# Attention weights turned by VectorE and transfers instead of TensorE, in a top-k attention and feed-forward kernel

## The chip, the cores and the metric

The kernel runs on one core of a Trainium2 chip. The metric is the device time of one execution in microseconds (us). PE is TensorE, DVE is VectorE, ACT is ScalarE, POOL is GpSimd, and SP is SyncE, which here only issues transfers. PEld is the weight load of PE.

## The reference

Attention with the 32 largest scores of each row, then a feed-forward block on its result:

```
B, H, S, D = 8, 8, 576, 64
scores = q @ k.T / 8                      # per batch and head, 576 x 576
kth    = 32nd largest score of the row
attn   = softmax(where(scores >= kth, scores, -1e9))
x      = (attn @ v), heads side by side   # 4608 x 512
h      = x @ w_in                         # 512 x 2048
out    = (h - tanh(h)) @ w_out            # 2048 x 512
```

q, k and v are float32. The two weight matrices lie in memory as float64, and the kernel turns them into float32 itself. All matmuls are float32.

## The kernel before

**Steps.** The attention is cut into 144 steps. A step (class Step: batch b, head pair hp, query tile qt) takes two heads and 128 query rows of each. A batch has 16 such steps (four head pairs, four query tiles) and two remainder steps (qt = 4, `rem`), in which the last 64 query rows of four heads share one tile. So a batch is 18 steps. The order is written out by hand in `plan`: the half a = 0 (query tiles 0 and 1 of all head pairs, eight steps), then the two remainder steps, then a = 1. Two steps with the same hp and neighbouring qt make a pair, and `values` works once per pair.

**What a step does.** `scores` makes scps with PE (L202) and copies it to sc with ACT (L210). `search` finds the 32nd largest on DVE: it folds the two halves of a row into a maximum and a minimum (L232, L233), and makes four rounds of MAX8 (L240) and MATCH_REPLACE8 (L243), three of the latter. `mask` computes the threshold on POOL (tbs L259, nb L268), subtracts a huge multiple of what lies below it (ACT L272, POOL L275), and keeps b8s (L277) for a test at the end of whether the fold lost anything. `expo` takes the exponential in place in z on ACT (L288) with its row sum den, and POOL adds a small number (rd L302). `invert` is the reciprocal on DVE (L309) once per pair, and `spread` widens it on POOL (rx L319).

**Turning the weights.** z has queries on the partitions; the product with v needs keys there. `weigh` does that on PE: eight 128 x 128 transposes into PSUM (zt L341), copied by ACT to et (L344), and one more for the last 64 keys of both heads (L347, copied to e4 by L348). `values` multiplies with v (av L368), transposes rx beside it (L376), copies both (xs L380) and multiplies them on POOL into the unit's xT (L390, or L385 for a remainder).

**Feed-forward.** A unit is 256 finished rows of x: two per batch, and one of remainder rows for every four batches, 18 in all. `values` of a unit's last step (dictionary `done`) puts the unit's work items on a list: 16 of `ffn_h` (hps L410; every second one followed by tanh L422, copy L423 and subtraction L424) and 16 of `ffn_o` (ops L430, copy ot L440, store L442). `deal` takes items from the list inside the loop over steps, in four places of a step, so many that the list is empty when the next unit is due (`share`).

**The loop.** Every engine works through its instructions in the order in which the loop writes them. Iteration n holds `weigh` for step n-2, `mask` for n-1, `search` for n, items, `scores` for n+1, the end of `weigh`, `expo` for n-1, items, `values` for n-2, items, and then loads (`todo`): k and q of the next head pair, turned by DVE in 32 x 32 blocks (`turn_kq` L186), and v (L176, L180).

**Converting the weight matrices.** In the first 17 steps (EARLY) `search` is interleaved with 32 pieces of `convert`. A piece is loaded twice by ACT's queue, as raw (L119) and with an offset as shifted (L121), three places each. Its first part is two operations on DVE (L131, L135) and three on ACT (L132, L133, L138); its second part is one on DVE (L141) and one on POOL (L144). After a piece's second part the piece three further on is loaded. `between(i)` is called after round i of a search and runs what is planned there: one piece per step in steps 0 to 8, four in step 9, three in the steps after it.

```
seq = [(1, i) for i in mine[:1]]
for i in mine[1:]:
    seq += [(1, i), (2, i - 1)]
seq += [(2, i) for i in mine[-1:]]
for x, (part, i) in enumerate(seq):
    parts.setdefault((m, 3 * x // max(len(seq) - 1, 1)), []).append((part, i))
```

Of the kernel before, what the change touches and what calls it, by code (L numbers as in the profile page):

```python
# [42 lines left out]
def kernel(  # L43
# [21 lines left out]
    NG = P // G  # L65
    WJ = 4
# [22 lines left out]
    rawpool = pool("raw", 3)  # L89
    shpool = pool("shifted", 3)  # L90
# [13 lines left out]
    NW = 512  # L104
    e1151 = consts.tile([P, 1], FP32, name="e1151")
# [4 lines left out]
    def convert(j, i):  # L110


        if j < WJ:
            src, dst = moe_w_in[i * P : (i + 1) * P, j * NW : (j + 1) * NW], w_in[j][:, i, :]
        else:
            r0 = ((j - WJ) * FJ + i) * P
            src, dst = moe_w_out[r0 : r0 + P, :], w_out[j - WJ][:, i, :]
        raw = rawpool.tile([P, NW, 2], U32, tag="raw", name="raw")
        nc.scalar.dma_start(raw[:].rearrange("p n w -> p (n w)"), src.bitcast(U32))  # L119
        shifted = shpool.tile([P, NW, 2], U32, tag="shifted", name="shifted")  # L120
        nc.scalar.dma_start(  # L121
            shifted[:].rearrange("p n w -> p (n w)").bitcast(U8)[:, 0 : 8 * NW - 4],
            src.bitcast(U8)[:, 3 : 8 * NW - 1],
        )
        yield
        hi = raw[:, :, 1]
        f = thpool.tile([P, NW], FP32, tag="th", name="f")
        fu = f[:].bitcast(U32)


        nc.vector.tensor_scalar(fu, hi, 20, 0x7FF, ALU.logical_shift_right, ALU.bitwise_and)  # L131
        nc.scalar.activation(f[:], fu, AF.Relu, bias=e1151[:], scale=-(2.0**23))  # L132
        nc.scalar.activation(f[:].bitcast(I32), f[:], AF.Relu, bias=e255[:], scale=-1.0)  # L133

        nc.vector.tensor_scalar(  # L135
            dst.bitcast(U32), shifted[:, :, 0], 0x0FFFFFFF, None, ALU.bitwise_and
        )
        nc.scalar.activation(dst, dst.bitcast(U32), AF.Copy, bias=1.0, scale=2.0**-28)  # L138
        yield

        nc.vector.scalar_tensor_tensor(  # L141
            out=fu, in0=hi, scalar=0x80000000, in1=fu, op0=ALU.bitwise_and, op1=ALU.bitwise_or
        )
        nc.gpsimd.tensor_tensor(dst, dst, f[:], ALU.mult)  # L144
        yield
# [101 lines left out]
    tbs = consts.tile([P, 2, B * NHP * J + 2 * B], FP32, name="tbs")  # L247
    b8s = consts.tile([P, 2, B * NHP * J + 2 * B], FP32, name="b8s")

    def mask(n, exact):  # L250
# [3 lines left out]
        scf = sc[:].rearrange("p t s k -> p t (s k)")  # L254
        if exact:
            nc.gpsimd.tensor_scalar(tbs[:, :, n], m[:, :, TOP - 1], BIG, None, ALU.mult)
        else:
            for t in range(2):
                nc.gpsimd.tensor_scalar(  # L259
                    tbs[:, t, n : n + 1],  # L260
                    m[:, t, TOP - 1 : TOP],
                    m[:, t, TOP - 9 : TOP - 8],
                    BIG,
                    ALU.min,
                    ALU.mult,
                )
# [4 lines left out]
        for t in range(2):  # L271
            nc.scalar.activation(  # L272
                zv[:, t, :], scf[:, t, :], AF.Relu, bias=tbs[:, t, n : n + 1], scale=-BIG
            )
            nc.gpsimd.tensor_tensor(zv[:, t, :], scf[:, t, :], zv[:, t, :], ALU.subtract)  # L275
        if not exact:
            nc.gpsimd.tensor_scalar(  # L277
                b8s[:, :, n], x.pop("ab")[:, :, S2 + 7], BIG, None, ALU.mult
            )
# [41 lines left out]
    ets = {}  # L321

    def weigh(n):


        g, z = steps[n], st[n]["z"]
        if g.rem:
            o = 0
        else:
            o = (g.qt % 2) * P  # L330
        if o:
            et, e4 = ets[n - 1]
        else:
            et = etpool.tile([P, 2, J, N], FP32, tag="et", name="et")
            e4 = etpool.tile([P, N], FP32, tag="e4", name="e4")
        ets[n] = et, e4
        for t in range(2):
            zt = zt_ps.tile([P, 512], FP32, tag="zt", name="zt")
            m0 = t * (S + R)
            for c in range(J):  # L340
                nc.tensor.transpose(  # L341
                    zt[:, c * P : (c + 1) * P], z[:, m0 + c * P : m0 + (c + 1) * P], ident[:]
                )
            nc.scalar.copy(et[:, t, :, o : o + P], zt[:].rearrange("p (c j) -> p c j", c=J))  # L344
        yield
        zt = zt_ps.tile([P, 512], FP32, tag="zt", name="zt")
        nc.tensor.transpose(zt[:, 0:P], z[:, JP : JP + P], ident[:])  # L347
        nc.scalar.copy(e4[:, o : o + P], zt[:, 0:P])  # L348
        st.pop(n)
        yield  # L350

    def values(n):
# [4 lines left out]
        et, e4 = ets.pop(n)  # L357
        ets.pop(n - 1, None)
        rx = rxs.pop(n)
        nq = 1 if g.rem else 2  # L360
        w = nq * P
        av = zt_ps.tile([P, 2, N], FP32, tag="zt", name="av")
        for i in range(2 if g.rem else 1):
            cols = half(i) if g.rem else slice(0, N)
            hp = g.hp + i
            for c in range(J + 1):
                for t in range(2):
# [3 lines left out]
                        et[:, t, c, cols] if c < J else e4[:, cols],  # L371
# [3 lines left out]
        for i in range(nq):  # L375
            nc.tensor.transpose(  # L376
                av[:, 1, i * P : (i + 1) * P], rx[:, i].rearrange("p t d -> p (t d)"), ident[:]
# [10 lines left out]
        else:  # L388
            u = units[g.b, g.qt // 2]
            nc.gpsimd.tensor_tensor(xt(u)[:, g.hp, :], xs[:, 0], xs[:, 1], ALU.mult)  # L390
# [65 lines left out]
    def plan():  # L456
# [8 lines left out]
        for b in range(B):  # L465
# [3 lines left out]
            for a in range(2):  # L469
# [3 lines left out]
                done[len(steps) - 1] = units[b, a]  # L473
                if a == 0:
                    steps.extend([Step(b, hp, J) for hp in range(0, NHP, 2)])
                    if b % 4 == 3:
                        done[len(steps) - 1] = rests[-1]

    def run(exact):
# [9 lines left out]
        for i, (b, hp) in enumerate(pairs):  # L489
            n = first[b] + 2 * hp  # L490
# [9 lines left out]
        many = {9: 4} | {n: 1 for n in range(9)} | {n: 3 for n in range(10, 17)}  # L500
        EARLY = 0 if exact else 17
        parts, started = {}, 0
        for m in range(EARLY):
# [8 lines left out]
        for piece in pieces[:3]:  # L512
            next(piece)
        converted = [0 if pieces else 2 * WJ * FJ]

        def between(i):
            for part, k in parts.pop((n, i), []):
                next(pieces[k])
                if part == 2:
                    converted[0] = k + 1  # L520
                    if k + 3 < len(pieces):
                        next(pieces[k + 3])
            if i == 0 and 0 <= n - 2 and n < EARLY:
                invert(n - 2)

# [11 lines left out]
        for n in range(-4, NS + 2):  # L537
            here = lambda i: 0 <= n + i < NS
            more = min([m + 2 for m in done if m + 2 >= n], default=n)
            share[0] = len(work) / (more - n + 1)  # L540
            if here(-2):
                if n >= EARLY:
                    spread(n - 2)
                w = weigh(n - 2)
                next(w)
# [4 lines left out]
            if here(-2) and n < EARLY:  # L550
                spread(n - 2)
# [3 lines left out]
            if here(-2):  # L555
                next(w)
            if here(-1):
                expo(n - 1)
                if n + 1 >= EARLY:
                    invert(n - 1)  # L560
            deal(0.2)
            if here(-2):
                values(n - 2)
# [14 lines left out]
    bad = xpool.tile([P, 2, NS], FP32, tag="bad", name="bad")  # L578
    nc.vector.tensor_tensor(bad[:], b8s[:], tbs[:], ALU.is_gt)
# [39 lines left out]
```

## Time and profile before

| | |
|---|---|
| three runs | 1695.82, 1696.7, 1698.19 us; median 1696.7 |
| profiled execution | 1698.08 us, of which the span is 1696.2 |
| mean granted clock of PE | 0.969 |
| busy: PE, DVE, ACT, POOL | 1559.7, 1202.8, 1020.0, 890.8 us |
| moved by transfers | 73.01 MB, mean 43 GB/s |
| first search starts | 20.56 us |
| last search starts | 1603.13 us |

The page shows one execution: busy time of each engine, the span in 40 slices (a digit is the busy share in tenths), and the chain of work that ended last. The start of a step is read from L232, the first operation of its search on DVE; there are 144 of them. A busy PE need not be at its peak, since matmuls overlap.

### The profile page before, as it was taken

Reading aid. Unit: us, or ns where it says so; the run is one execution under the profiler, and the core shown is the slowest. Engines: PE = TensorE matmul, PEld = TensorE weight load, DVE = VectorE, ACT = ScalarE, POOL = GpSimd, SP = SyncE. Lnnn points to the kernel's source line nnn. Section 1 sums busy time; section 2 is a strip of 40 time slices with the busy share of each in tenths; the row PEclk is TensorE's granted clock in tenths of the full one; section 3 lists DMA queues with packets and bytes.
Section 4 is the critical chain, followed back from the end, with each engine's and each line's share of the span. In section 5 each row is a group of like instructions: output and inputs, shape, how many; then the busy total and the mean of one; then the engine's idle time right before and its main releaser. Section 6 shows DMA issues by size and latency. Waiting matters only on the chain.

```text
span 1696.2 us, 24926 instructions
## 1 busy us (share of the span) xinstructions
PE 1559.7 (92%) x8098; PEld 1007.6 (59%) x8098; DVE 1202.8 (71%) x3699; ACT 1020.0 (60%) x1941; POOL 890.8 (53%) x1373
## 2 busy tenths in 40 slices
PE   1555569999999999999999999999999999999998
PEld 0334435757575757575656575757575757575664
DVE  5877888877887888743787788778887888733700
ACT  2676666757665766643656576657675766643631
POOL 1555565646564655543646464647564656543620
PEclk9867779999999999999999999999999999999999
DMA  6524442200220013000131002100220022000000
GB/s 161 135 99 174 180 149 54 37 14 1 49 49 7 8 34 57 13 7 13 18 59 22 14 8 55 36 14 1 49 49 7 8 41 43 7 7 13 1 13 15
DMA packets 205068, 73.01 MB, mean 43 GB/s; under 512 B 192128, under 2 KB 192128, under 8 KB 204928
## 3 DMA queue, kind: packets, MB, share of 16 engines
q1 hardware_dynamic: 195712, 37.78, 11.1%
q10 hardware_dynamic: 9216, 33.54, 5.6%
q8 instruction: 66, 1.08, 0.3%
q14 instruction: 74, 0.61, 0.1%
HBM read 61.85 MB, written 9.44 MB: 42 GB/s over the span
## 4 chain that ended last, share of the span: by engine, by line
PE 86%; DVE 7%; ACT 3%; DMA 1%; issue 1%; ACTq 1%; POOL 1%; SPq 0%; DVEq 0%; POOLq 0%
PE ops L430 29%; PE hps L410 28%; PE av L368 9%; PE scps L202 9%; PE zt L341 7%; DVE m L240 2%; PE zt L347 2%; DVE ab L243 2%; PE av L376 2%; DVE f L141 1%; ACT sc L210 1%; ACT z L272 1%; DMA kin<-in_k_dram 1%; DVE w_out L135 0%; DVE ab L232 0%
## 5 line engine op out<-in xcount | busy, mean ns | idle before, releaser
L275 POOL TENSOR_TENSOR z<-sc,z 128x576 f32<-128x576 f32 x288 | 401.9, 1417 | 238.2 <-ACT z L272 238.1
L430 PE MATMUL ops<-w_out,g 128*128 128x512 f32 x1152 | 524.6, 596 | 0.0
L410 PE MATMUL hps<-xT,w_in 128*128 128x256 f32 x2048 | 472.8, 383 | 0.0
L240 DVE MAX8 m<-ab 128x8 f32<-128x288 f32 (+1 forms) x1152 | 468.1, 448 | 0.0
L410 PEld LDWEIGHTS hps<-xT,w_in 128*128 128x128 f32 x2048 | 386.1, 194 | 47.4 <-issue 0.5
L243 DVE MATCH_REPLACE8 ab<-m,ab 128x288 f32<-128x288 f32 x864 | 375.9, 443 | 0.0
L430 PEld LDWEIGHTS ops<-w_out,g 128*128 128x128 f32 x1152 | 210.8, 194 | 199.9 <-issue 198.2
L424 POOL TENSOR_TENSOR g<-g,th 128x512 f32<-128x512 f32 x144 | 183.4, 1273 | 184.9 <-ACT g L423 181.9
L272 ACT ACTIVATE z<-sc,tbs 128x576 f32<-128x576 f32 x288 | 208.3, 775 | 51.4 <-POOL tbs L259 51.4
L210 ACT COPY sc<-scps 128x1152 f32<-128x1152 f32 x144 | 160.2, 1113 | 128.3 <-ACT z L272 46.5
L288 ACT ACTIVATE z<-z,nb 128x576 f32<-128x576 f32 x288 | 222.7, 779 | 15.1 <-POOL z L275 15.1
L344 ACT COPY et<-zt 128x512 f32<-128x512 f32 x288 | 156.9, 598 | 114.3 <-PE zt L341 114.1
L202 PE MATMUL scps<-kT,qT 64*128 64x288 f32 (+1 forms) x1280 | 188.7, 448 | 28.4 <-DVE qT L186 16.8
L341 PE MATMUL zt<-ident,z 128*128 128x128 f32 x1152 | 160.1, 285 | 49.4 <-ACT z L288 48.6
L341 PEld LDWEIGHTS zt<-ident,z 128*128 128x128 f32 x1152 | 141.8, 147 | 96.2 <-ACT z L288 54.7
L422 ACT ACTIVATE th<-hps 128x512 f32<-128x512 f32 x144 | 85.2, 592 | 160.1 <-PE hps L410 141.5
L309 DVE RECIPROCAL rd<-rd 128x4 f32<-128x4 f32 x64 | 11.3, 177 | 237.9 <-POOL rd L302 237.9
L202 PEld LDWEIGHTS scps<-kT,qT 64*128 64x128 f32 (+1 forms) x1280 | 101.5, 184 | 122.0 <-issue 38.1
L232 DVE TENSOR_TENSOR ab<-scps,sc 128x576 f32<-128x576 f32 x144 | 105.7, 734 | 81.1 <-ACT sc L210 74.8
L368 PE MATMUL av<-et,vb 128*64 128x256 f32 (+1 forms) x1536 | 146.9, 335 | 0.0
L368 PEld LDWEIGHTS av<-et,vb 128*64 128x64 f32 x1536 | 86.7, 139 | 61.3 <-ACT e L348 12.9
L235 DVE MAX8 ab<-ab 128x8 f32<-128x288 f32 x288 | 116.2, 444 | 0.0
(53 smaller groups left out, 1228.2 us busy)
## 6 DMA issues: line engine op xcount, KB each, us to landing
kin<-in_k_dram SPq DMA_DIRECT2D x128, 72.0 KB, 2.4
qin<-in_q_dram SPq DMA_DIRECT2D x128, 72.0 KB, 2.4
raw<-in_moe_w_in_dram ACTq DMA_DIRECT2D x16, 512.0 KB, 3.6
vb<-in_v_dram SPq DMA_DIRECT2D x64, 128.0 KB, 2.5
raw<-in_moe_w_out_dram ACTq DMA_DIRECT2D x16, 512.0 KB, 3.8
out_dram<-ot SPq DMA_DIRECT2D x32, 256.0 KB, 2.0
shifted<-in_moe_w_in_dram ACTq DMA_DIRECT2D x16, 511.5 KB, 5.0
shifted<-in_moe_w_out_dram ACTq DMA_DIRECT2D x16, 511.5 KB, 4.7
```

What stands on the lines that cost most here:

```text
L202: nc.tensor.matmul(ps[rows, t, s, 0:S2], qT[g.b, g.hp + i][half(t), qs], kT[g.b, g.hp + i][half(t), ks], start=True, stop=True,)
L210: nc.scalar.copy(sc[:], ps[:, :, :, 0:S2])
L240: nc.vector.max(m[:, t, m8], last[t] if i == rounds - 1 else cur[t])
L243: nc.vector.match_replace(nxt[t], m[:, t, m8], cur[t], NEG)
L272: nc.scalar.activation(zv[:, t, :], scf[:, t, :], AF.Relu, bias=tbs[:, t, n : n + 1], scale=-BIG)
L275: nc.gpsimd.tensor_tensor(zv[:, t, :], scf[:, t, :], zv[:, t, :], ALU.subtract)
L288: nc.scalar.activation(x["zv"][:, t, :], x["zv"][:, t, :], AF.Exp, bias=x["nb"][:, t : t + 1], scale=scale, accum_out=den[:, t : t + 1],)
L341: nc.tensor.transpose(zt[:, c * P : (c + 1) * P], z[:, m0 + c * P : m0 + (c + 1) * P], ident[:])
L368: nc.tensor.matmul(av[half(t), 0, cols], vb[g.b, hp][:, t, c, :] if c < J else vr[g.b, hp][:, t, :], et[:, t, c, cols] if c < J else e4[:, ...
L410: nc.tensor.matmul(ps[:, f % 2, :], w_in[j][:, c, fo : fo + P], u.xT[:, c, :], start=(c == 0), stop=(c == CD - 1),)
L424: nc.gpsimd.tensor_tensor(g, g, th[:], ALU.subtract)
L430: nc.tensor.matmul(cur[u][:], u.g[f // FJ][:, f % FJ, i * P : (i + 1) * P], w_out[f // FJ][:, f % FJ, :], start=(f == 0), stop=(f == CF - 1),)
```

## The change

The weights are turned by DVE in 32 x 32 blocks (`turn_z`), 1152 columns of one step at a time, into one of two places zx. The blocks then stand in the wrong partition groups, so `spread_keys` moves them with 16 transfers on SP per pair (or remainder), each from 32 partitions to 32 partitions in runs of 2304 bytes (1152 for a remainder), into et, of which there is one. PE's transposes and ACT's copies of them are gone. The columns of et have another order, which `values` undoes in its access patterns. `turn_z` of step n-2 stands in the search of step n: after round 0 from step 21 on, and before that after round 0 for the second step of a pair, after round 3 for the first, and after round 1 for a remainder.

The second zx lies over the memory in which raw and shifted are loaded, and is used from step 17 on; raw and shifted have two places each instead of three, and after a piece's second part the piece two further on is loaded. The reciprocal of step n-2 stands in the search of step n for all steps. `spread` works on n-3, and `values` on n-4 at the head of an iteration. The remainder steps are spread over the half a = 1 (a = 0 in the last batch). The test at the end keeps one byte per row, made by two POOL operations a step instead of one.

The diff, cut to its core:

```diff
-    rawpool = pool("raw", 3)
-    shpool = pool("shifted", 3)
...
+    EARLY = 17
+    spare = consts.tile([P, 4, NW, 2], U32, name="spare")
+    zx2 = [
+        consts.tile([P, 4 * S], FP32, name="zx")[:],
+        spare[:].rearrange("p a n w -> p (a n w)").bitcast(FP32)[:, 0 : 4 * S],
+    ]
...
-        raw = rawpool.tile([P, NW, 2], U32, tag="raw", name="raw")
+        raw = spare[:, i % 2]
...
-        shifted = shpool.tile([P, NW, 2], U32, tag="shifted", name="shifted")
+        shifted = spare[:, 2 + i % 2]
...
         if not exact:
-            nc.gpsimd.tensor_scalar(
-                b8s[:, :, n], x.pop("ab")[:, :, S2 + 7], BIG, None, ALU.mult
-            )
+            ab = x.pop("ab")
+            for t in range(2):
+                nc.gpsimd.tensor_scalar(
+                    bad[:, t, n : n + 1], ab[:, t, S2 + 7 : S2 + 8], BIG, tb[:, t : t + 1],
+                    ALU.mult, ALU.is_gt,
+                )
...
-    def weigh(n):
...
-        for t in range(2):
-            zt = zt_ps.tile([P, 512], FP32, tag="zt", name="zt")
-            m0 = t * (S + R)
-            for c in range(J):
-                nc.tensor.transpose(
-                    zt[:, c * P : (c + 1) * P], z[:, m0 + c * P : m0 + (c + 1) * P], ident[:]
-                )
-            nc.scalar.copy(et[:, t, :, o : o + P], zt[:].rearrange("p (c j) -> p c j", c=J))
-        yield
-        zt = zt_ps.tile([P, 512], FP32, tag="zt", name="zt")
-        nc.tensor.transpose(zt[:, 0:P], z[:, JP : JP + P], ident[:])
-        nc.scalar.copy(e4[:, o : o + P], zt[:, 0:P])
...
+    def turn_z(n):
+        g, z = steps[n], st.pop(n)["z"]
+        i = 0 if g.rem else g.qt % 2
+        if not i:
+            zxs[n] = zx2[1 if n >= TWO and last_zx[0] == 0 else 0]
+            last_zx[0] = 0 if zxs[n] is zx2[0] else 1
+        else:
+            zxs[n] = zxs[n - 1]
+        zx = zxs[n]
+        zv, _ = tiles(zx, n)
+        nc.vector.transpose(
+            zv[:, :, :, i, :].rearrange("p c k j -> p k c j"),
+            z[:].rearrange("p (k c j) -> p k c j", c=NG, j=G),
+        )
+
+    def spread_keys(n):
+        zx = zxs.pop(n)
+        zxs.pop(n - 1, None)
+        et = ets[n] = etpool.tile([P, 4 * S], FP32, tag="et", name="et")
+        w = tiles(et, n)[1] * S // 2
+        for a in range(NG):
+            for c in range(NG):
+                nc.sync.dma_start(
+                    et[group(c), a * w : (a + 1) * w], zx[group(a), c * w : (c + 1) * w]
+                )
...
-                done[len(steps) - 1] = units[b, a]
-                if a == 0:
-                    steps.extend([Step(b, hp, J) for hp in range(0, NHP, 2)])
-                    if b % 4 == 3:
-                        done[len(steps) - 1] = rests[-1]
+                    if hp == NHP - 1:
+                        done[len(steps) - 1] = units[b, a]
+                    if hp % 2 and a == (b < B - 1):
+                        steps.append(Step(b, hp - 1, J))
+                        if hp == NHP - 1 and b % 4 == 3:
+                            done[len(steps) - 1] = rests[-1]
...
+        def turn_at(n):
+            g = steps[n]
+            return 0 if n >= TWO + 2 else 1 if g.rem else 3 - 3 * (g.qt % 2)
...
-                    if k + 3 < len(pieces):
-                        next(pieces[k + 3])
-            if i == 0 and 0 <= n - 2 and n < EARLY:
+                    if k + 2 < len(pieces):
+                        next(pieces[k + 2])
+            if here(-2) and i == 0:
                 invert(n - 2)
+            if here(-2) and i == turn_at(n - 2):
+                turn_z(n - 2)
...
-            more = min([m + 2 for m in done if m + 2 >= n], default=n)
-            share[0] = len(work) / (more - n + 1)
+            more = min([m + 4 for m in done if m + 4 > n], default=n)
+            if here(-4):
+                values(n - 4)
+            share[0] = len(work) / max(more - n, 1)
+            if here(-3):
+                spread(n - 3)
             if here(-1):
                 mask(n - 1, exact)
             if here(0):
                 search(n, exact, between)
...
+            if here(-2) and last_of_pair(n - 2):
+                spread_keys(n - 2)
             deal(0.4)
```

## The prediction

> **What bounds the kernel now.** I read first the page (engine totals, slices, chain), then a table of windows, the list of waits, and last the timelines of single engines.
>
> ```profile
> PE 1559.7 (92%) x8098; PEld 1007.6 (59%) x8098; DVE 1202.8 (71%) x3699; ACT 1020.0 (60%) x1941; POOL 890.8 (53%) x1373
> PE   1555569999999999999999999999999999999998
> PEclk9867779999999999999999999999999999999999
> PE 86%; DVE 7%; ACT 3%; DMA 1%; issue 1%; ACTq 1%; POOL 1%; SPq 0%; DVEq 0%; POOLq 0%
> ```
>
> There are two stages. Up to about 260 us PE is half idle; from there to the end it is full, and the chain runs through it. Two windows (PE, PEld, DVE, ACT, POOL busy, clock, DMA share, GB/s) and one line of the waits (total us, times, longest) say the same:
>
> ```profile
> 180.00:200.00 20.00, 12.00 (x57) 9.68 (x57) 14.77 (x36) 13.51 (x27) 12.62 (x15) 0.84 0.42 160
> 1200.00:1400.00 200.00, 200.00 (x1071) 126.55 (x1070) 163.52 (x514) 131.70 (x253) 114.25 (x186) 1.00 0.16 31
> ```
> ```profile
> DVE rd L309 <- POOL rd L302: 237.9, 57, 17.1
> ```
>
> In the full stage DVE is 82% busy and sits at its reciprocal until PE's backlog lets the next step through. So there a microsecond taken from PE counts, until DVE is full too.
>
> **The sizes per step.** The chain in order of time, late in the run, prices PE's work without gaps:
>
> ```profile
> 1574.28 0.87 PE zt L341 x8
> 1576.88 1.17 PE scps L202 x8
> 1578.05 0.26 PE zt L347
> 1589.25 2.31 PE av L368 x20
> 1633.48 27.63 PE hps L410 x128
> 1661.11 27.48 PE ops L430 x64
> ```
>
> The change drops L341 and L347: 0.87 + 0.26 = 1.13 us a step, 163 us over 144 steps (the chain's 7% + 2% of the span say 153). A feed-forward unit is 27.6 + 27.5 = 55.1 us. A batch is 18 steps: the starts of L232 at 363.0 (step 27) and 539.25 (step 45) make it 176.2 us, all PE. Without transposes PE needs 176.2 - 18 x 1.13 = 156 us a batch.
>
> Now DVE, from its timeline:
>
> ```profile
> 1006.17 0.73 DVE L232 TENSOR_TENSOR ab<-scps,sc 128x576 f32<-128x576 f32 x1
> ...
> 1013.66 0.76 DVE L186 STREAM_TRANSPOSE kT<-kin 128x576 f32<-128x576 f32 x1
> 1014.35 0.72 DVE L232 TENSOR_TENSOR ab<-scps,sc 128x576 f32<-128x576 f32 x1
> ```
>
> An undisturbed search is 1013.66 - 1006.17 = 7.49 us and a 576-column turn delays the next operation by 0.69 us. The new turn has 1152 columns. Bounds from that row: 0.69 (if the column count did not matter) to 1.38 (two of them); most of the row's time must be columns, so I take 1.3. Its output is written in runs of 32 words with strides, which no turn here shows; L131 reads every second word, 512 in 0.34 us, so strides are cheap in that row. A batch on DVE then takes 18 x (7.49 + 1.3) = 158.2, plus eight k and q turns of 0.69 = 5.5, plus ten reciprocals of 0.09 = 0.9: 164.6 us. I take 166.5 for semaphore instructions of the new waits (21 to 35 ns each at L186, up to eight before a turn, mostly issued ahead). DVE (166.5) passes PE (156) and is the next bound. The gain per batch is 176.2 - 166.5 = 9.7 us, not 20.
>
> **ACT and POOL.** ACT loses two L344 copies and one L348, 0.6 + 0.6 + 0.27 = 1.47 us a step, of 7.1: in the full stage worth nothing, ACT is no bound. POOL trades one b8s (0.27) for two, the xT product gets a permuted view (0.73 now); it has 6.2 us a step and 9 to spend. Nothing, while DVE's 9 us cover it; uncovered, 0.3 us x 144 = 43. The later reciprocal removes the 237.9 us wait, but this was PE's backlog showing there: with PE relieved, DVE's own work is late next. It and the rx copy now have a whole step before values, moved to n-4, needs them.
>
> **The transfers.** A pair issues 16 of them on SP, 72 KB each. Nearest rows, from the DMA issues (KB each, us to landing) and SP's timeline:
>
> ```profile
> kin<-in_k_dram SPq DMA_DIRECT2D x128, 72.0 KB, 2.4
> ```
> ```profile
> 74.01 2.07 SPq L164 DMA_DIRECT2D qin<-in_q_dram  x4
> ```
>
> Four issues take 2.07 us of SP, a landing 2.4, and issues overlap. At 0.37 (an output store) to 0.58 (vb) each, 16 hold SP 6 to 9 us; I take 0.5, 8 us. The turn ends some 5.6 us into step m+2, the last transfer lands at 5.6 + 8 + 2.4 = 16 us, and values(m) stands at the head of m+4, 17.6 us later. PE may be some 1.3 us late there before DVE feels it (values, xs 0.59, the xT product 0.73, tbs and nb 0.85, two L272 1.44, sc 1.13 in line must fit in a step). So they are hidden for an issue cost up to (18.9 - 8.0)/16 = 0.68 us. Queued behind the waiting SP are k, q and v loads and output stores; they have more than a step before their readers. The remainder steps are tighter: there is one et, so their transfers wait for the previous values and have one step; PE waits about 3 us for 16 of them, inside the 10 us a batch that PE has over.
>
> One rule speaks against this. The Trainium skill, "DMA: Bandwidth & Descriptors", Rules for kernel authors, says that transfers near 64 KB are mostly overhead, and its section Anatomy of one DMA gives 2.0 us plus bytes over 436 GB/s, so 2.2 us for 72 KB. One after the other, 16 of these would be 35 us a pair and the kernel would go to about 64 x 35 + 16 x 34 = 2780 us. The k and q row above shows that the fixed part overlaps, so I follow the row.
>
> **The early stage (steps 0 to 17).** Here DVE and ACT pass the turn to each other, and the change costs time. First, an odd step's turn stands after round 0: steps 3, 5 and 7 get 1.3 us each, 4 us. An even step's turn stands at the end, where DVE waits 2.11 us for sc anyway: free. Second, raw and shifted have two places, not three. In steps 9 to 15 the third piece's loads are issued right after piece one is finished, and its first conversion is the next instruction on DVE (step 12 on DVE's and ACT's timelines, and the landing):
>
> ```profile
> 187.90 0.43 DVE L131 TENSOR_SCALAR f<-raw 128x512 uint32<-128x512 uint32 x1
> 188.24 1.50 DVE L135 TENSOR_SCALAR w_out<-shifted 128x512 uint32<-128x512 uint32 x1
> ```
> ```profile
> 188.01 0.33 ACTq L119 DMA_DIRECT2D raw<-in_moe_w_out_dram  x1
> 188.38 0.45 ACTq L121 DMA_DIRECT2D shifted<-in_moe_w_out_dram  x1
> ```
> ```profile
> shifted<-in_moe_w_out_dram ACTq DMA_DIRECT2D x16, 511.5 KB, 4.7
> ```
>
> The loads issued at 188.0 and 188.4 now feed DVE's 187.9 and 188.2: it would wait until 188.4 + 4.7 = 193.1, so about 4 us a step, 28 over seven. The dropped ACT copies (1.47 a step) bring the first piece forward; I take +20, bounds 0 and +40. Steps 16 and 17 (23.9 us, PE's backlog) become about 20. Step 18, now at 273.4, starts at 273.4 + 4 + 20 - 4 = 293.
>
> **The sum.** Six batches (steps 18 to 125): 293 + 6 x 166.5 = 1292. After batch 3 the remainder unit ends one step behind another unit, and the share then deals a whole 55.1 us unit in one step: DVE idles about 55.1 - 9 = 46, giving 1338 (before has such a place too, steps 64 to 66 with 20.5, 29.4, 24.8). Step 138 starts 111 us on (10 steps of 8.8, two more, eight turns), at 1449. From there PE alone: the second such unit with its values and scores 59; the last remainder unit 55.1, values 1.6 + 3 x 2.7 and four scores 4.7, 70; the last values and their way through ACT and POOL 4; the last unit 55.1; the end as now, 1696.2 - 1688.6 = 7.6. Span 1449 + 59 + 70 + 4 + 55 + 8 = 1645. The profiled execution was 1698.1 for a span of 1696.2, and the median of the runs is 1.4 below it, so the prediction is 1645 + 1.9 - 1.4 = 1645.5, written 1646.
>
> **The rivals.**
> Wash: DVE's batch at 172 instead of 166.5 (stalls from PE's uneven load) is +33, the early bound +20 more: 1646 + 53 = 1699. For it: both engines are within 7% of each other. Against: before never starves PE in the same loop.
> Slower, the turn is dear: if strided output doubles 1.3 to 2.6, then 144 x 1.3 = +187, 1833. It decides from 1.3 + 50/144 = 1.65 us per turn.
> Slower, late transfers: above 0.68 us an issue PE stands at values. At 0.8: 64 pairs x 1.9 + 16 remainders x 4 = 186, 1832. Against it stand all SP rows, 0.37 to 0.58.
> Better: no early loss and 164.6 a batch: 1646 - 20 - 11 = 1615.
> That the change does not do what it says is no real rival: the built order has no transposes of z left on PE.
>
> A clock rival is small. The slices show the clock at 0.7 while PE waits 6 to 11 us a step before 260 us, and 1.00 after. The Trainium skill, "TensorE: Matmul & The Clock Gate", Part 1, has the gate close after an idle window of about 3.4 us; the waits I expect later are shorter, and if the 16 remainder waits did close it, some 3.4 us each would be 54 us of PE, partly inside its reserve.
>
> **How the numbers follow.** Forecast (1620 to 1692) 0.56, better 0.08, wash 0.14, dear turn 0.08, late transfers 0.14. About 0.2%, 3.4 us, is what a measurement can tell from no change. Faster gets the forecast, better, and 0.03 of the wash: 0.67; same 0.06; slower 0.27. The range takes in the better case and the wash: 1605 to 1715.
>
> **What would show it.** Right: L341, L344, L347, L348 gone; DVE the largest share of the chain after 300 us; starts of the search 8.8 to 9.6 us apart; PE 93 to 97% in the full stage at clock 1.00; DVE idle behind raw and shifted in steps 9 to 15. Wrong: a turn over 1.65 us; PE's av waiting on DMA for more than 3 us at most pairs; a batch over 176 us.

## The result, and the profile after

| | before | after |
|---|---|---|
| median of the runs | 1696.7 us | 1709.2 us (1705.4 to 1712.5, 4 runs) |
| after / before | | 1.0072, 95% interval 1.0047 to 1.0097 |
| profiled execution, span | 1698.1, 1696.2 us | 1712.5, 1710.7 us |
| step 18 starts | 273.4 us | 320.7 us (forecast 293) |
| batches (18 steps) from step 18 | 174.7, 176.2, 226.9, 181.5, 176.2, 176.2 | 171.6, 170.0, 172.4, 219.9, 173.6, 172.2 (forecast 166.5, one with 46 more) |
| steps 126 to 137 | 150.2 us | 115.6 us (forecast 111) |
| from step 138 to the end | 160.8 us | 194.7 us (forecast 196) |

Slower by 0.7%, where a gain of 3% was forecast. The miss in the span is 1710.7 - 1645 = 65.7 us, and it splits by the forecast's own terms: 27.7 before step 18, 34.7 in the six batches (1079.7 against 1045), 4.6 in steps 126 to 137, and -1.3 at the end.

From the page of the changed kernel: engine totals, the slices of PE and of its clock, the chain.

```profile
PE 1444.8 (84%) x6802; PEld 886.7 (52%) x6802; DVE 1384.2 (81%) x3842; ACT 857.9 (50%) x1509; POOL 942.8 (55%) x1517
PE   1232444899998999899999999899899999899998
PEclk9956767999999999999999999999999999999999
PE 53%; DVE 15%; SPq 14%; DMA 7%; issue 4%; ACT 4%; POOL 2%; ACTq 1%; DVEq 0%; POOLq 0%
```

The change did what it says: PE lost 115 us, DVE gained 181. But the chain is not DVE's, as it would be if DVE were the bound. It runs through SP's queue (14%) and transfers (7%), which carried 1% before. A window of the full stage (columns as in the prediction) has PE and DVE at 96% each, neither of them full, and the clock at 0.98:

```profile
400.00:600.00 200.00, 191.84 (x917) 112.61 (x915) 192.48 (x553) 110.42 (x197) 122.67 (x206) 0.98 0.39 89
```

Four lines of the waits (total us, times, longest) name what stood between:

```profile
DVE ab L240 <- POOL bad L287: 66.7, 26, 31.6
PE av L393 <- DMA et<-zx: 41.7, 16, 5.4
DVE kT L194 <- DMA kin<-in_k_dram: 29.9, 15, 14.3
DVE f L139 <- DMA spare<-in_moe_w_out_dram: 20.2, 5, 4.6
```

**One stall, followed.** SP's timeline around step 56 (start, us, operation):

```profile
667.38 11.35 SPq L374 DMA_DIRECT2D et<-zx  x16
678.77 2.26 SPq L172 DMA_DIRECT2D kin<-in_k_dram  x4
681.13 2.06 SPq L172 DMA_DIRECT2D qin<-in_q_dram  x4
683.31 10.01 SPq L374 DMA_DIRECT2D et<-spare  x16
...
696.34 3.25 SPq L172 DMA_DIRECT2D kin<-in_k_dram  x4
699.69 2.06 SPq L172 DMA_DIRECT2D qin<-in_q_dram  x4
701.86 10.05 SPq L374 DMA_DIRECT2D et<-zx  x16
```

The row of 16 transfers (a train) at 683.31 is that of the remainder (step 53). Its turn ended at 676.8, but two things held it until 683.3: loads of k and q on SP ahead of it, to 683.2, and the one et, which PE's `values` of the pair before reads until 683.1 (PE's timeline):

```profile
682.45 0.63 PE L393 MATMUL av<-et,vr 128*64 128x256 f32 x4
```

The loads of v, k and q queue behind this train, and the train of steps 54 and 55 behind them: turned at 698.1, it starts at 701.86, and its last transfer is issued at 711.9. With 2.0 us to landing et is there at 713.9. PE needed it at 711:

```profile
713.99 3.53 PE L393 MATMUL av<-et,vb 128*64 128x256 f32 x16 [3.01 <-DMA vb<-in_v_dram]
```

The row names v's load. But the v issued in these microseconds (711.96) is that of a later pair, and this pair's was issued at 662.6; so it is et. The 16 matmuls take 3.53 us where those of the next pair (733.06) take 1.95, and the clock beside them (the number before the last two) is 0.50:

```profile
713.80:717.20 3.40, 3.21 (x16) 2.10 (x18) 3.40 (x10) 0.00 (x0) 0.00 (x0) 0.50 0.60 112
```

Then ACT's xs (718.4), POOL's product, tb, z and bad follow in line, and DVE waits:

```profile
724.28 0.76 DVE L240 TENSOR_TENSOR ab<-scps,sc 128x576 f32<-128x576 f32 x1 [3.42 <-POOL bad L287]
```

The line of the waits says "POOL bad", but POOL is only the last of a chain that begins at SP. In each batch such stalls lie behind the remainders (whose `values` come in steps 34, 52, 70 and so on) and in the half that loads k and q. Step 19 takes 12.1 us and step 37 11.0, with DVE at kT, since k's load stands behind a train. In step 55 that is the train at 667.38 above:

```profile
682.94 0.78 DVE L194 STREAM_TRANSPOSE kT<-kin 128x576 f32<-128x576 f32 x1 [2.27 <-DMA kin<-in_k_dram]
```

In the other half most steps take 8.78 or 8.83 us, as forecast (8.8).

### The profile page after: what moved, and what is told of

It reads as the page before. It is cut to its first block, busy times and chain, and to the rows that moved or that the text cites. A ratio compares the mean times of both kernels' runs of the same rounds, so it can differ in the third digit from the quotient of the medians.

```text
span 1710.7 us, 24180 instructions
## 1 busy us (share of the span) xinstructions
PE 1444.8 (84%) x6802; PEld 886.7 (52%) x6802; DVE 1384.2 (81%) x3842; ACT 857.9 (50%) x1509; POOL 942.8 (55%) x1517
## 4 chain that ended last, share of the span: by engine, by line
PE 53%; DVE 15%; SPq 14%; DMA 7%; issue 4%; ACT 4%; POOL 2%; ACTq 1%; DVEq 0%; POOLq 0%
PE hps L442 20%; PE ops L462 19%; SPq L374 12%; PE av L393 7%; PE scps L210 6%; DVE m L248 3%; DVE ab L251 3%; DMA spare<-in_moe_w_out_dram 2%; SPq L172 2%; DMA spare<-in_moe_w_in_dram 2%; DVE zx L360 1%; DMA kin<-in_k_dram 1%; DVE f L149 1%; DVE ab L240 1%; DVE ab L243 1%
## 5 line engine op out<-in xcount | busy, mean ns | idle before, releaser
L442 PE MATMUL hps<-xT,w_in 128*128 128x256 f32 x2048 | 484.2, 392 | 56.2 <-ACT g L455 38.4
L442 PEld LDWEIGHTS hps<-xT,w_in 128*128 128x128 f32 x2048 | 390.7, 195 | 137.7 <-ACT g L455 41.5
L462 PEld LDWEIGHTS ops<-w_out,g 128*128 128x128 f32 x1152 | 214.7, 193 | 256.8 <-issue 249.5
L280 ACT ACTIVATE z<-sc,tb 128x576 f32<-128x576 f32 x288 | 207.6, 768 | 200.5 <-POOL tb L267 200.5
L240 DVE TENSOR_TENSOR ab<-scps,sc 128x576 f32<-128x576 f32 x144 | 106.8, 742 | 151.7 <-ACT sc L218 84.7
L393 PE MATMUL av<-et,vb 128*64 128x256 f32 (+1 forms) x1536 | 157.6, 351 | 65.1 <-DMA et<-zx 41.7
L393 PEld LDWEIGHTS av<-et,vb 128*64 128x64 f32 x1536 | 93.9, 145 | 143.7 <-issue 100.5
L417 POOL TENSOR_TENSOR xT<-xs 128x256 f32<-128x256 f32 x64 | 48.3, 754 | 185.7 <-ACT xs L405 180.8
L405 ACT COPY xs<-av 128x512 f32<-128x512 f32 (+1 forms) x80 | 43.4, 543 | 212.4 <-PE av L401 212.4
L360 DVE STREAM_TRANSPOSE zx<-z 128x1152 f32<-128x1152 f32 x80 | 108.7, 1359 | 0.0
L241 DVE TENSOR_TENSOR ab<-scps,sc 128x576 f32<-128x576 f32 x144 | 107.6, 747 | 0.0
```

The lines of the kernel that those rows point to most:

```text
L280: nc.scalar.activation(zv[:, t, :], scf[:, t, :], AF.Relu, bias=tb[:, t : t + 1], scale=-BIG)
L393: nc.tensor.matmul(av[half(t), 0, cols], vb[g.b, hp][:, t, c, :] if c < J else vr[g.b, hp][:, t, :], es[:, :, (J + 1) * t + c if c < J els ...
L442: nc.tensor.matmul(ps[:, f % 2, :], w_in[j][:, c, fo : fo + P], u.xT[:, c, :], start=(c == 0), stop=(c == CD - 1),)
L462: nc.tensor.matmul(cur[u][:], u.g[f // FJ][:, f % FJ, i * P : (i + 1) * P], w_out[f // FJ][:, f % FJ, :], start=(f == 0), stop=(f == CF - 1),)
```

## The experiments

The medians are of four to ten runs, with the kernel before run beside them; ratios are to the kernel before, with 95% intervals. "Steps 9 to 15" and so on are read from the starts of the search.

### The early stage: e1, e2, e8

**e1_three_load_places.**

```diff
+    third = w_out[WJ - 1][:].rearrange("p a n -> p (a n)").bitcast(U32)
+    places = [(spare[:, 0], spare[:, 2]), (spare[:, 1], spare[:, 3]), (third[:, 0], third[:, 1])]
-        raw = spare[:, i % 2]
+        raw = places[where[j * FJ + i]][0]
...
+            if waiting and (place < 2 or waiting[0] < 26):
```

> The changed kernel with one thing undone: raw and shifted have three places again (the third one lies in the fourth block of w_out, which is free until piece 26), so a piece is loaded two parts earlier. Theory (a), the two load places cost the early stage most of its loss: steps 9 to 15 take about 140 to 150 us instead of 167.1, step 18 starts at about 285 to 298 instead of 320.7, the whole is 22 to 35 us shorter than the changed kernel (about 1675 to 1687). Rival (b), the early loss comes from the turn and from POOL's and DVE's collisions in steps 2 to 8 and from ACT's loads behind SP's transfers: step 18 stays above 312 and the whole within 10 us of 1709. In both, steps 2 to 8 stay near 91 us and the later batches near 172.

1691.5 us, 0.997 (0.9957 to 0.9983). Steps 9 to 15 took 143.5 us instead of 167.1, the rest stayed. Theory (a) holds by these steps; step 18 at 298.7 and the whole lie a little outside its ranges. The profiled executions differ by 22.7 us and the medians by 17.7; single runs of one kernel spread by 7 us and more. Of the 13.4 us that still separate steps 9 to 15 from before's 130.1, 12.1 are in steps 14 and 15, where the third place is already needed for w_out.

**e2_before_two_places.**

```diff
-    rawpool = pool("raw", 3)
-    shpool = pool("shifted", 3)
+    rawpool = pool("raw", 2)
+    shpool = pool("shifted", 2)
...
-                    if k + 3 < len(pieces):
-                        next(pieces[k + 3])
+                    if k + 2 < len(pieces):
+                        next(pieces[k + 2])
```

> The kernel before with one part of the change alone: two places for raw and for shifted, the next piece loaded after the second part of the piece two earlier. Theory (a), the load places are what costs the early stage: step 18 starts 25 to 37 us later than before's 273.4, and the whole takes about 1718 to 1733. Rival (b): under 10 us, since DVE's waits for a load are hidden by PE's own work; the whole stays below 1707.

1721.1 us, 1.0143 (1.0126 to 1.0159): +24.7, and 26.3 in steps 9 to 15. This part of the change alone costs the kernel before 1.4%.

**e8_first_part_later.**

```diff
-                parts.setdefault((m, 3 * x // max(len(seq) - 1, 1)), []).append((part, i))
+                slot = 1 if m < 9 and x == 0 else 3 * x // max(len(seq) - 1, 1)
+                parts.setdefault((m, slot), []).append((part, i))
```

> The changed kernel with the first part of a weight piece one round of the search later in steps 0 to 8 (after round 1 instead of round 0), nothing else. Theory (g), in steps 2 to 8 DVE's first two operations of a piece take 1.41 and 1.62 us instead of about 0.45 because POOL's z runs at the same time, which the order of the change brought about: moved away they fall below 0.6 us on average and steps 2 to 8 take 83 to 86 us instead of 91.2, the whole 4 to 9 us less. Rival (h), the 14 us there are the turn (7 at 1.3 us, 9 us) and waits: steps 2 to 8 stay above 89 us, the whole within 3 us of 1709.

1703.4 us, 1.0031 (1.0019 to 1.0043); steps 2 to 8 took 83.8 us instead of 91.2. The groups of DVE between 42 and 128 us (times | busy us, mean ns), in the order before, after, e8:

```profile
L135 DVE TENSOR_SCALAR w_in<-shifted 128x512 uint32<-128x512 uint32 x9 | 3.8, 421 | 0.0
```
```profile
L143 DVE TENSOR_SCALAR w_in<-spare 128x512 uint32<-128x512 uint32 x7 | 8.9, 1277 | 0.0
```
```profile
L143 DVE TENSOR_SCALAR w_in<-spare 128x512 uint32<-128x512 uint32 x9 | 3.8, 418 | 0.0
```

The same operation takes three times as long in the changed kernel, and its old time when it stands a round later: (g) for w_in. The other one, L139, went from 1033 only to 727 ns (before: 518, as L131), so (g)'s "below 0.6" failed there. In step 6 POOL's two z run from 95.66 to 98.60, and DVE's pair from 95.94 ends at 98.89. 6.7 us over before remain: odd steps take 12.3 us here, 1.3 more than before, even ones 11.4 to 11.8, 0.4 to 0.8 more.

### The full stage: what makes et late

**e5_four_transfers.**

```diff
-        for a in range(NG):
-            for c in range(NG):
-                nc.sync.dma_start(
-                    et[group(c), a * w : (a + 1) * w], zx[group(a), c * w : (c + 1) * w]
-                )
+        for c in range(NG):
+            nc.sync.dma_start(et[group(c), 0 : NG * w], zx[group(c), 0 : NG * w])
```

> The changed kernel with 4 transfers for a pair instead of 16, from partition group c to the same group c, of the same bytes in runs of 9216; the exchange between the groups is left out, so this only measures what the number of issues costs. Theory (d), SP's issues (16 at about 0.63 us) make et, v and k late: the waits of DVE behind bad and behind k's load both fall below a third (from about 30 and 12 us in steps 18 to 125), the batches come to 165 to 167 us, the whole is 25 to 45 us shorter (1664 to 1684). Theory (c), the order on ACT and POOL: the batches keep 170 us or more and the whole is within 12 us of 1709. In the early stage fewer transfers should save little in both (step 18 at 310 to 321).

1661.3 us, 0.9794 (0.9778 to 0.981). Batches: 163.7, 163.7, 163.7, 216.2, 163.6, 164.8, and the chain is now DVE's:

```profile
DVE 55%; PE 26%; DMA 6%; issue 5%; ACT 4%; POOL 2%; ACTq 1%; SPq 0%; DVEq 0%; POOLq 0%
```

So with four issues for 16 the loss of the full stage is gone, and DVE's own sum (164.6) was right. The bytes are the same; a transfer takes 5.1 us to landing instead of 2.0, but a train is out after four issues. This kernel leaves out the exchange between the groups: it prices the issues and does not do the work.

**e3_product_behind_mask** and **e10_values_later** change the order instead.

```diff
-        xs = xrpool.tile([P, 2, N], FP32, tag="xs", name="xs")
+        avs[n] = av, nq, w
+    def product(n):
+        av, nq, w = avs.pop(n)
+        xs = xrpool.tile([P, 2, N], FP32, tag="xs", name="xs")
...
                 mask(n - 1, exact)
+            if here(-4):
+                product(n - 4)
```

> The changed kernel with ACT's copy xs and POOL's product xT of step n-4 moved behind the mask of step n-1; PE's values stay at the head. Theory (c), the steady stage loses its 5 to 6 us a batch because the chain PE values, ACT xs, POOL xT stands ahead of the mask's tb, z and bad on POOL, for which the search two steps on waits: DVE's waits for bad (66.7 us, of which about 30 in steps 18 to 125) fall below 10 us there, a batch takes 166 to 168 us instead of 172, and the whole is 20 to 35 us shorter (1675 to 1690). Rival (d), SP's issues are the cause (0.63 us each, so v, k and et come late): the waits move from bad to another place (kT behind its load, sc, the product) and the batches stay at 170 to 173, the whole within 10 us of 1709.

1769.5 us, 1.0433 (1.0415 to 1.0452). DVE's waits for bad in steps 18 to 125 fell from 30.9 to 6.8 us, as (c) said, but those for sc rose from 35.2 to 108.8, and a batch took 177. The wait moved, and grew; neither theory's total came. Why PE's scores came so late there was not tried further.

```diff
-            if here(-4):
-                values(n - 4)
             share[0] = len(work) / max(more - n, 1)
...
                 scores(n + 1)
+            if here(-4):
+                values(n - 4)
```

> The changed kernel with the whole of values of step n-4 moved from the head of the iteration to behind scores of n+1, so that PE, ACT and POOL do the next search's scores and the mask first; SP's queue as it is. Theory (i), the stall comes where values stands at the head and its wait for et blocks PE before scores: with about 3 us more before it waits, the stalls behind bad (3.4, 2.9, 1.9 us) vanish, those behind k's load stay (about 12 us over six batches apart from the two dumps), a batch takes 166 to 169 us, the whole 1675 to 1695. Rival (j), et is then freed 3 us later, SP's next 16 transfers start later by the same, and the lateness goes round: batches of 172 us or more.

1771.5 us, 1.0438 (1.042 to 1.0455): (j). A batch took 179; DVE's waits for k in steps 18 to 125 rose from 26.9 to 89.1 us. et is freed later, the train starts later, and k's load behind it too.

**e7_kqv_loads_on_act**, **e5b_half_on_act** and **e9_v_loads_on_pool** take issues off SP.

```diff
-    def load_kq(b, hp):
+    def load_kq(b, hp, queue=nc.sync):
...
+                at(n - 2, lambda i=i, n=n: load_kq(*pairs[i + 1], nc.scalar if n >= 20 else nc.sync))
+            at(n - 1, lambda b=b, hp=hp, n=n: load_v(b, hp, nc.scalar if n >= 20 else nc.sync))
```

> The changed kernel with the loads of k, q and v issued on ACT's queue instead of SP's from step 20 on; the 16 transfers of a pair stay on SP with all their bytes. Theory (d'), SP is full in the half of a batch that loads k and q (16 at 0.63, 8 at 0.52, 4 at 0.58 and a store are 17 to 18 us of a pair's 18.9): with some 6.5 us of a pair taken off SP the waits behind bad and behind k's load fall below a third, a batch takes 164 to 167 us, and the whole is 28 to 48 us shorter than 1709 (1661 to 1681). Rival (e), the 16 transfers are late by themselves, whatever stands beside them: batches stay at 170 to 173, within 10 us of 1709. Rival (f), the loads cost on ACT what they saved on SP: waits behind ACT's sc appear, a batch takes 168 to 172.

```diff
-                nc.sync.dma_start(
+                (nc.scalar if c % 2 and n > 20 and not steps[n].rem else nc.sync).dma_start(
```

> The changed kernel with every second of a pair's 16 transfers issued on ACT's queue (pairs from step 21 on, not the remainders). Theory (d'): SP has about 5 us of a pair less, its fullest pairs take 12 to 13 of 18.9 us, a batch takes 164 to 168 us and the whole 1665 to 1685. Rival (f), ACT stands behind the turn and its copies xs and sc come late: waits behind ACT's sc, batches of 170 us or more, the whole 1700 or more.

1812.1 us, 1.0678 (1.066 to 1.0696), and 1851.5 us, 1.0913 (1.0895 to 1.0932). Both are slower, as (f) said, and e7 by far more than it said (168 to 172): the batches take 185 to 194, apart from the one with a whole unit. In e7 DVE's waits grew most at bad (99.0 us in steps 18 to 125, from 30.9), less at sc (53.1, from 35.2). ACT's timeline of e5b shows the price:

```profile
704.33 5.02 ACTq L374 DMA_DIRECT2D et<-zx  x8
709.45 1.12 ACT L218 COPY sc<-scps 128x1152 f32<-128x1152 f32 x1 [5.79 <-DMA et<-zx]
```

Eight issues hold ACT for 5 us, with sc, which DVE's next search needs, behind them. An issue is not free of the engine that makes it.

```diff
-            at(n - 1, lambda b=b, hp=hp: load_v(b, hp))
+            at(n - 1, lambda b=b, hp=hp, n=n: load_v(b, hp, nc.gpsimd if n >= 20 else nc.sync))
```

> The changed kernel with the four loads of v for a pair issued on POOL's queue from step 20 on, instead of SP's. Theory (d'): SP's 17 to 18.4 us of issues for a pair of 18.9 become 15 to 16, so late transfers are made up for sooner: DVE's waits for bad and k fall to about half, a batch takes 167 to 170 us instead of 172, the whole 1680 to 1700. Rival (f'), an issue takes POOL's own time as it took ACT's in the run with k, q and v there, and bad is late for it: a batch takes 172 us or more, the whole 1709 or more.

1714.9 us, 1.011 (1.0094 to 1.0127). An issue takes POOL 0.55 to 0.99 us. 2.3 us less on SP for each pair gained nothing: batches 172.1, 171.6, 173.1, as (f') said. As POOL paid for the issues, this alone does not settle whether SP's total is the cause; e19 does, where SP keeps every issue and most of the loss is gone. What stays is when a train may start, and what lies behind it.

**e14_own_et_for_rest**, **e17_k_load_earlier**, and both: **e19_own_et_and_k_load**.

```diff
+    etr = spare[:].rearrange("p a n w -> p (a n w)").bitcast(FP32)[:, 4 * S : 6 * S]
...
+        if steps[n].rem and n >= EARLY:
+            et = ets[n] = etr
```

> The changed kernel with an et of their own for the remainder steps from step 17 on (in the part of the memory of raw and shifted that the second zx leaves free); issues, order and bytes as they are. Theory (k), one et and a train of 10 us: the stalls behind bad after a remainder and after the first pair that follows it (2.9, 1.9, 1.0, 3.4, 1.6 us, and the long steps before them) vanish, a batch takes 165 to 168 us instead of 172, the whole 1675 to 1692. Rival (l), what is queued on SP decides: under 8 us of gain, 1701 or more, and k's waits stay or grow.

```diff
+            if i + 1 < len(pairs):
+                at(n - 3, lambda i=i: load_kq(*pairs[i + 1], "k"))
             at(n - 2, lambda turn=turn: next(turn))
             if i + 1 < len(pairs):
-                at(n - 2, lambda i=i: load_kq(*pairs[i + 1]))
+                at(n - 2, lambda i=i: load_kq(*pairs[i + 1], "q"))
```

> The changed kernel with k's load issued one step earlier (right after the turn of the k before it, so ahead of the next train), q's as it is. Theory (l): DVE's waits for k, 12 us over six batches, vanish and with them 2 us a batch and what follows from them: the whole 1690 to 1700. Theory (k): k's waits vanish but the stalls behind bad take their place: 1703 to 1712.

> The changed kernel with both late transfers mended (own et for the remainders, k's load a step earlier) and the early stage as the change made it. Alone they gave 8.7 and 4.3 us. If each hides the other: 1709 less 25 to 35, 1674 to 1684, a batch of 165 to 166. If they only add: 1694 to 1698, a batch of about 169.

| | us | ratio | batches |
|---|---|---|---|
| after | 1709.2 | 1.0072 (1.0047 to 1.0097) | 171.6, 170.0, 172.4, 219.9, 173.6, 172.2 |
| e14: own et | 1700.5 | 1.0029 (1.0019 to 1.004) | 169.9, 169.5, 170.4, 218.5, 169.3, 170.9 |
| e17: k earlier | 1704.9 | 1.0041 (1.0025 to 1.0056) | 169.4, 168.9, 171.4, 219.5, 174.1, 172.4 |
| e19: both | 1675.0 | 0.9875 (0.9858 to 0.9891) | 164.3, 165.3, 165.9, 217.7, 169.0, 166.5 |

Alone 8.7 and 4.3 us, together 34.2; the 4.3 is hardly clear of noise, as the two intervals overlap. With an own et DVE still waited for k (35.0 us in steps 18 to 125, 26.9 before that edit); with k earlier the waits for k were down to 2.8, but those for bad were 24.7 (from 30.9). Of each sum for k but the 2.8, some 14 us lie in step 75, where PE is at the whole unit; with k earlier DVE waits there for sc instead. Two late transfers stood side by side, and each kept the step late when the other was mended. Step 35 shows it: after has two waits (first two rows), e14 only that for k (third), longer than it was; e17 has 3.89 us at the search; e19 has none.

```profile
481.56 0.76 DVE L240 TENSOR_TENSOR ab<-scps,sc 128x576 f32<-128x576 f32 x1 [2.88 <-POOL bad L287]
491.56 0.78 DVE L194 STREAM_TRANSPOSE kT<-kin 128x576 f32<-128x576 f32 x1 [1.14 <-DMA kin<-in_k_dram]
488.99 0.78 DVE L194 STREAM_TRANSPOSE kT<-kin 128x576 f32<-128x576 f32 x1 [2.45 <-DMA kin<-in_k_dram]
```

With its own et the remainder's train at the same place of the batch (SP at 680.33 in e14) still starts right behind the loads of k and q, as the two ends at 683.1 and 683.2 above let expect. Neither (k) nor (l) was right alone; e14 and e17 by themselves looked like two small causes and not like the answer.

### The reciprocal: e18_before_later_reciprocal

```diff
-            if i == 0 and 0 <= n - 2 and n < EARLY:
+            if i == 0 and here(-2):
                 invert(n - 2)
...
-                if n + 1 >= EARLY:
-                    invert(n - 1)
```

> The kernel before with the reciprocal of step n-2 in the search of n for all steps, and nothing else of the change. If DVE's 237.9 us before the reciprocal are PE's backlog: the wait moves to another line (sc or ab of the next search) and the whole stays within 6 us of 1697. If the reciprocal itself held DVE back: 1680 or less.

1696.5 us, 1.000 (0.9991 to 1.001). The kernel before waited 237.9 us at the reciprocal; here the same wait stands at the search:

```profile
DVE ab L232 <- POOL b8s L277: 238.3, 94, 15.5
```

### Put together: e6, e11, e12, e15, e16

> Three edits on the changed kernel together: three load places as in e1, the first part of a piece a round later as in e8, and the loads of k, q and v on ACT's queue from step 20 on as in e7. If SP's issues and the load places are the two causes and add up: 1709 - 18 - 5 - 40, so 1640 to 1655, 2.5 to 3.3% under the kernel before. If the loads only move a wait to ACT: 1675 to 1690.

> The changed kernel with three load places (e1) and the first part of a piece a round later in steps 0 to 8 (e8), nothing on the queues. Measured alone they gave 17.7 and 5.8 us. If they add up: 1709.2 - 23.5, so 1683 to 1689 and 0.6 to 0.8% under the kernel before. If they overlap (the early stage runs into PE's or ACT's own limit): 1690 to 1694.

> The kernel with three load places and the later first part, and values behind scores as well. By theory (i): 1686 less 15 to 35, so 1650 to 1672. By rival (j): 1686 or more.

> Three load places, the later first part, and an et of their own for the remainders: by theory (k) 1682.5 less 17 to 34, so 1648 to 1666; by (l) 1675 to 1684.

> As the kernel with three places, later part and own et, and k's load one step earlier as well. If k's load is still late there: 8 to 15 us under that kernel. If the own et has already made it harmless: within 3 us of it.

| | us | ratio |
|---|---|---|
| e6: e1, e8, k, q and v on ACT | 1786.0 | 1.0519 (1.0501 to 1.0537) |
| e12: e1, e8, values later | 1742.9 | 1.0271 (1.0256 to 1.0285) |
| e11: e1, e8 | 1682.5 | 0.9918 (0.9904 to 0.9932) |
| e15: e11 and own et | 1675.7 | 0.987 (0.9855 to 0.9885) |
| e16: e15 and k earlier | 1649.5 | 0.973 (0.9716 to 0.9743) |

e11 gained 26.7 us on the changed kernel, a little more than its parts' 23.5. e6 and e12 repeat the losses of e7 and e10; e6 lies far outside both of its ranges, e12 where (j) put it. e15 gained 6.8 on e11 where (k) said 17 to 34 (it lies in the range of (l)), and e16 another 26.2, far over the "8 to 15": the same pair of waits as in e19. e16 is 2.7% under the kernel before, the best of all. A window of it:

```profile
300.00:450.00 150.00, 143.62 (x739) 90.44 (x738) 148.58 (x423) 88.89 (x158) 100.51 (x168) 1.00 0.40 90
```

DVE is 99% busy and the clock is 1.00 here; from 1000 to 1400 us it is 0.98 to 0.99, with DVE at 98%. Step 18 starts at 291.8, the batches take 165.4, 165.4, 166.2, 217.6, 168.9, 167.8.

## Why the prediction was wrong, by its own steps

- **The change of bound, DVE's sum, the reciprocal.** Right. The turn takes 1.36 us, the next operation starts 1.3 later, undisturbed steps take 8.78 to 9.49 us, and e5 ran at 163.7 a batch against a sum of 164.6. The reciprocal as PE's backlog is shown by e18.
- **PE's 1.13 us a step.** Too much. Beside a DVE that is full (e5) PE is busy 160.4 to 161.2 us in a batch, against 176.2 before: 0.83 to 0.88 us a step less (115 us in the totals of the two pages, where 163 was forecast). So PE has some 3 us a batch over, not 10. As DVE is the bound, the total does not show it.
- **The remainder's wait.** This step failed. "PE waits about 3 us for 16 of them, inside the 10 us a batch that PE has over" has the wait about right: in steps 18 to 125 PE waits for et in 11 of 12 remainders, 2.7 us in the mean. The price was wrong. The same paragraph says that PE may be 1.3 us late at `values` before DVE feels it. The wait of a batch's first remainder (2.1 to 4.7 us) came out at DVE in the next step in all six batches, with 1.0 to 3.5 us. That of the second mostly did not, but in three batches PE then waited 2.1 to 3.2 us for the next pair's et, and DVE 1.9 to 3.9 behind it. A reserve counts only if it lies between the wait and the next reader.
- **"k, q and v loads ... have more than a step before their readers."** Wrong for k, and the second step that failed. By the order of the code k's load of iteration n-2 is turned in n-1, one step later. The remainder shifts the pairs by a step, so that twice in a batch a pair's train stands right ahead of that load, and DVE waits at kT. A train took 10.0 us, not 8 (0.63 an issue, taken 0.5, above the rows' 0.37 to 0.58). The limit of 0.68 us an issue was worked out for one pair on an empty queue and did not bear on either wait.
- **Their share.** Of the 34.7 us in the batches (profiled executions) e14 takes back 11, e17 4, and e19 31: the two steps together, hardly either alone.
- **The clock.** The prediction called it small because the waits would be shorter than 3.4 us. In steps 18 to 125 the profile's clock record has nine stretches at 0.5, of 3.4 or 6.8 us, 41 us in all. Each lies at a PE wait for et of 2.1 to 4.7 us, so the 3.4 us of idling that the prediction took for the gate were not needed here. Before has none, e5 has 3.4 us of them, e19 10. So a wait cost more than its length: in the stall above `values` took 3.96 us instead of 2.38 behind a wait of 3.01. What it is worth in the whole was not tried alone.
- **The early stage, load places.** Mechanism right (raw and shifted, the words of "what would show it"), size wrong: taken +20, bounds 0 and 40, steps 9 to 15 came to +37.0. The two places alone are 26.3 of it in e2, and e1 gives back 23.6. The 28 worked out from the landing row was nearer than the 20 after the discount for ACT's copies, which nothing in the profile had priced. The other 11 to 13 us had no term in the prediction. In e1 12.1 of them lie in steps 14 and 15, and no run says how much of that is the places and how much the turns of these steps.
- **The early stage, turns.** Taken +4, it was +14.1 in steps 2 to 8. Half of it (7.5, e8) is DVE held while POOL's z runs, which no step of the prediction had. That z comes earlier because ACT's copies no longer stand ahead of the mask is what the order of the code suggests; it was not tried alone. The other 6.7 fit the turns: the 1.3 of the odd steps was right, "free" for the even ones was wrong (0.4 to 0.8).
- **The rivals.** The result lies between forecast and "late transfers", near the wash's 1699, which had 0.14. The wash's 172 a batch was measured, but by late transfers and not by PE's uneven load. All of "forecast" rested on waits that would stay hidden in two places at once. With e1, e8, the own et and the earlier k the numbers of the sum come: step 126 at 1343 (forecast 1338), step 138 at 1453 (1449), 1649.5 against 1646. In part that is luck: this kernel has three load places, and still starts step 18 at 291.8, where the forecast had 293 with two.
- **The rule that spoke against.** The trains land in 2.0 us and overlap, as the k and q rows said, so the sum of 2780 us was far off. The Trainium skill, "DMA: Bandwidth & Descriptors", Rules for kernel authors, advises one large transfer in place of many small ones, and that pointed the right way: fewer and larger transfers were worth 48 us (e5), through the time of an issue and not through that of a landing. The prediction took that page loosely: the rule speaks of transfers under 64 KB and the formula is given for those that GpSimd issues, where these are 72 KB on SP.

## What to carry to other kernels

Where a wait is said to hide, find the next reader of what waits, and compare the wait with the time to that reader, not with the engine's spare time in a batch. A row of transfers on one queue has a length (issues times 0.6 us here) that counts for its buffer and for all that is queued behind it. When one repair gains little, look for a second wait that ends at the same place: 8.7 and 4.3 us apart were 34.2 together.

## What the runs showed of the hardware

- Moving issues from SP to ACT cost more than it saved: eight issues held ACT 5.02 us, in line with its copies. On POOL an issue took 0.55 to 0.99 us.
- Four transfers of 288 KB land in 4.7 to 5.1 us, sixteen of 72 KB in 2.0 each. Their issues take 2.4 to 3.8 us and 10.0, so that the same bytes are through after 7.5 to 8.5 and after 12 us: an issue of the larger ones is not cheaper (0.6 to 0.95 us), there are only fewer.
- DVE's plain 128x512 operation took 1277 instead of 421 ns beside POOL's z. The Trainium skill, "SBUF — State Buffer", section "SBUF: two separate sides", says that VectorE and GpSimd share a pair of ports as an exclusive lock, held for a whole instruction; of VectorE's operations it names those in a mode that uses both ports or with two inputs in SBUF. The times of step 6 fit, and e8 moved the operation away from it. Which instruction held the lock, and in which mode this one ran, was not measured.
- PE waits of 2.1 to 4.7 us were followed by 3.4 or 6.8 us at a granted clock of 0.5, nine times in steps 18 to 125. In windows of 200 us from 400 us on this reads as 0.97 to 0.98 (1.00 where the whole unit is dealt), in e16 as 0.98 to 1.00.
